# Two attention blocks on one core: a fixed order of work, B features read from PSUM, reciprocals by Ln and Exp, the first x tile turned on TensorE

## The chip, the cores and the metric

The kernel runs on one core of a Trainium2 chip. A time is device microseconds of that core, from the launch to the end; medians are of all runs of a series. A span is the profiled execution from its first to its last instruction, and is about 2 us shorter than the time of the same run. Some runs are marked slow (over 1.5% above the fastest run of the same kernel); ratios leave them out.

## The reference, cut to what matters

```python
def _A_ref(x, wqkv, wo):             # sliding window of 256, 32 heads of 20
    qkv = (x @ wqkv) ...             # B=1, S=2048, D=640
    scores = einsum("bhqd,bhkd->bhqk", q, k) * (Dh ** -0.5)
    mask = (i - j >= 0) & (i - j < 256)
    p = softmax(where(mask, scores, -1e9)); o = p @ v
    return o.reshape(B, S, D) @ wo

def _B_ref(x, wqkv, wo):             # linear attention, same sizes
    phi = lambda t: where(t > 0, t + 1, exp(t)) + 1e-6
    pq, pk = phi(q), phi(k)
    kv = einsum("bhsd,bhse->bhde", pk, v);  z = einsum("bhsd->bhd", pk)
    num = pq @ kv;  den = pq . z + 1e-6
    return (num / den).reshape(B, S, D) @ wo
# out = concatenate([A, B], -1), bf16
```

Block A needs 78 large exps of 128x2048 on ScalarE ("units" below), each fed by score matmuls into four PSUM banks (SC) and followed by mask products and P V matmuls. Block B is projections and small products. Its independent work is meant to fill TensorE while A waits.

## The kernel before

Every piece of work is an `op` with the engines that could run it. When the kernel is built, a greedy planner with a rough cost for each op chooses which engine runs what, and in which order each engine's stream is written. The parts that the change touches:

```python
# a group of matmuls into one of four PSUM banks FB[0..3]; the last op of evac gives the bank back
def group(mms, evac, key, ...): ...
def either(n): return {"DVE": dve_ps(n), "ACT": act_t(n)}     # planner's choice

# B features: copy out of PSUM, then exp and the max from SBUF
group(mms, [(either(HALF), lambda e, ps: copy(e, R1v[:, tb, ...], ps[:, 0:HALF]), ...)])   # x2 per block
def phi(dst, n, key, after, tag):
    # ACT:  e1 = exp(dst)
    # DVE:  e1 = min(e1, 1) + 1e-6                (tensor_scalar)
    # DVE:  dst = max(dst + 1 + 1e-6, e1)         (scalar_tensor_tensor)
    ...                                           # [cut]

# B denominators: VectorE add, four small transfers through DRAM, VectorE reciprocal
tensor_scalar_add(out=dsB, in0=ps, scalar1=1e-6)
dma d1 <- dsB[0:P:4];  dma rc <- d1;  reciprocal(rd, rc);  dma d2 <- rd;  dma rB <- broadcast(d2)

# x tiles: five transposing loads each, issued by the sync queue
q.dma_start_transpose(out=X[slot][:, c, :], in_=xsrc[which][t*NX:(t+1)*NX, c, :])

# masks: planner's choice
pl.op({"POOL": 0.25 + 0.002*4*w, "DVE": dve_sb(4*w)}, em, ...)
# [cut: everything else]
```

The softmax here doesn't subtract the row's maximum and nothing guards it: scores larger than these inputs give would overflow.

## Time and profile before

| | before |
|---|---|
| median time | 321.6 us (five runs, 318.5 to 327.2; 320.35 of three at the time of the prediction) |
| first exp starts / last exp ends | 25.96 / 283.79 us |
| busy: TensorE, VectorE, ScalarE, GpSimd | 264, 242, 198, 128 us |

First the page: busy time of the engines, then the busy share of TensorE, VectorE and ScalarE in 40 equal slices, in tenths.

```profile
PE 264.1 (82%) x4969; PEld 154.5 (48%) x5000; DVE 242.0 (76%) x495; ACT 197.9 (62%) x183; POOL 127.9 (40%) x150
...
PE   5257999979988878999989998986868687979593
...
DVE  7515565679998888658668268999999999987553
ACT  1004768648888877667775747888768875743100
```

Next the table of windows: start and end of a stretch, its length, then busy us and number of instructions for TensorE, its weight loads, VectorE, ScalarE and GpSimd, then granted clock, transfer share and GB/s. The first three stretches are head, middle and tail, cut at the first and the last exp; the last four are the part in which B's queries are made.

```profile
core 0: us, PE busy (x) PEld busy (x) DVE busy (x) ACT busy (x) POOL busy (x), PEclk, DMA share, GB/s
0.00:25.96 25.96, 13.00 (x56) 5.17 (x57) 11.96 (x29) 2.93 (x5) 11.54 (x28) 0.67 0.83 180
25.96:283.79 257.83, 223.80 (x4599) 130.87 (x4629) 209.49 (x420) 189.90 (x165) 106.90 (x105) 0.98 0.44 102
283.79:320.50 36.71, 27.33 (x316) 18.45 (x314) 20.58 (x47) 5.12 (x13) 9.43 (x18) 0.92 0.28 99
200.00:220.00 20.00, 16.44 (x319) 8.63 (x322) 19.45 (x39) 17.21 (x17) 8.56 (x9) 1.00 0.23 41
220.00:240.00 20.00, 15.18 (x302) 7.75 (x304) 19.96 (x37) 14.64 (x18) 11.85 (x11) 1.00 0.18 48
240.00:260.00 20.00, 15.66 (x434) 9.22 (x441) 19.97 (x43) 16.66 (x15) 9.43 (x11) 0.91 0.34 114
260.00:280.00 20.00, 16.70 (x417) 9.81 (x418) 19.36 (x40) 14.52 (x12) 10.45 (x12) 1.00 0.24 87
```

No engine bounds the whole span. In the middle TensorE has the most work (224 of 258 us), but in the last four rows VectorE is at 97 to 100% and TensorE at 76 to 84%.

The chain of waits, in order of time (start, length, what it was), shows the head: nine transposing loads, each issued by the sync queue (SPq) in 1.2 to 1.3 us, one after the other, then weights.

```profile
0.81 1.25 SPq L357
...
12.52 3.56 DMA R<-in_A_x_dram
...
16.10 5.54 DMA WV<-in_A_wqkv_dram
```

From the grouped view, the lines that the change removes or alters. After the bar: busy us, mean ns of one; after the second bar: the idle time of the engine just ahead of them, and who ended it.

```profile
L490 ACT ACTIVATE P<-SC 128x2048 bf16<-128x2048 f32 x78 | 146.4, 1877 | 51.0 <-PE SC L483 45.8 <-POOL P L513 3.5 <-issue 0.6
...
L319 DVE CAST R<-F 128x320 bf16<-128x320 f32 x35 | 16.6, 481 | 7.5 <-PE F L625 4.6 <-PE F L660 2.7
...
L653 DVE SCALAR_TENSOR_TENSOR R<-R,E 128x640 bf16<-128x640 bf16 x16 | 15.2, 947 | 0.1
...
L653 DVE SCALAR_TENSOR_TENSOR R<-R,E 128x512 bf16<-128x512 bf16 x10 | 8.9, 901 | 0.0
```

The large exps waited 45.8 us for scores. The SBUF form of the max (scalar-tensor-tensor) took 0.95 us for 640 elements in the mean. Of the 35 copies in the second line some are of output rows (those that waited for L625); these stay.

### The profile page before, as it was taken

What the parts mean: (1) busy time and instruction counts of PE and PEld (TensorE: products, weight loads), DVE (VectorE), ACT (ScalarE), POOL (GpSimd) and SP (SyncE); (2) the same over time, 40 slices, a digit from 0 to 9 for tenths busy, and PEclk for the clock granted to TensorE, in tenths of its full rate; (3) what the DMA queues carried; (4) which work ended last, traced back from release to release, by engine and by line L of the source; (5) the groups of instructions that cost most, each with busy time, mean ns of one, the idle gap of its engine ahead of it and who ended that gap; (6) DMA issues with size and microseconds to landing.
All of it is one profiled execution on the core that took longest, in us unless ns stands there. A gap on an engine that the chain in (4) does not pass through costs nothing.

```text
span 320.5 us, 11419 instructions
## 1 busy us (share of the span) xinstructions
PE 264.1 (82%) x4969; PEld 154.5 (48%) x5000; DVE 242.0 (76%) x495; ACT 197.9 (62%) x183; POOL 127.9 (40%) x150
## 2 busy tenths in 40 slices
PE   5257999979988878999989998986868687979593
PEld 1024454537544445565655864543435354546362
DVE  7515565679998888658668268999999999987553
ACT  1004768648888877667775747888768875743100
POOL 9500132430144535643435324272754564423232
PEclk9559999979999999999999979999999899999978
DMA  5896451844944541063509599400304222243221
GB/s 118 164 234 139 118 92 19 188 94 125 192 95 99 110 78 39 10 162 76 120 18 179 139 314 134 69 21 20 104 14 158 84 92 83 88 142 128 95 85 82
DMA packets 63028, 34.63 MB, mean 108 GB/s; under 512 B 52406, under 2 KB 59190, under 8 KB 62966
## 3 DMA queue, kind: packets, MB, share of 16 engines
q1 hardware_dynamic: 56194, 25.38, 35.2%
q0 software_dynamic: 1536, 5.24, 4.5%
q10 hardware_dynamic: 5248, 3.28, 4.3%
q8 instruction: 39, 0.64, 0.9%
q14 instruction: 11, 0.09, 0.1%
HBM read 15.50 MB, written 10.58 MB: 81 GB/s over the span
## 4 chain that ended last, share of the span: by engine, by line
DVE 39%; PE 30%; DMA 9%; issue 9%; SPq 6%; ACT 4%; POOL 2%; POOLq 0%; DVEq 0%; ACTq 0%
PE F L396 6%; PE F L424 6%; DMA RB<-RD 5%; PE F L660 5%; DVE RB L603 4%; DVE E L652 4%; PE F L669 4%; PE F L625 4%; DVE R L653 4%; ACT P L490 4%; SPq L357 4%; DVE P L513 3%; PE SC L483 3%; DVE ON L319 3%; DVE OT L604 3%
## 5 line engine op out<-in xcount | busy, mean ns | idle before, releaser
L490 ACT ACTIVATE P<-SC 128x2048 bf16<-128x2048 f32 x78 | 146.4, 1877 | 51.0 <-PE SC L483 45.8
L513 POOL TENSOR_TENSOR P<-P,MK 128x512 bf16<-128x512 bf16 (+1 forms) x90 | 98.6, 1105 | 147.2 <-ACT P L490 145.1
L483 PE MATMUL SC<-QK 20*64 20x128 bf16 (+4 forms) x1600 | 33.6, 253 | 4.7 <-ACT P L490 4.2
L513 DVE TENSOR_TENSOR P<-P,MK 128x512 bf16<-128x512 bf16 (+1 forms) x58 | 27.8, 486 | 5.9 <-ACT P L490 5.5
L660 PE MATMUL F<-W,X 128*128 128x320 bf16 x160 | 25.7, 313 | 4.8 <-DVE R L319 2.5
L729 PE MATMUL F<-X,XT 128*128 128x512 bf16 x94 | 23.9, 381 | 6.7 <-DVE G L319 1.5
L483 PEld LDWEIGHTS <-QK 20*64 20x64 bf16 x1600 | 15.6, 104 | 27.1 <-issue 25.9
L319 DVE CAST R<-F 128x320 bf16<-128x320 f32 (+1 forms) x43 | 22.0, 518 | 8.5 <-PE F L625 4.6
L572 PE MATMUL F<-P,V 64*32 64x64 bf16 (+4 forms) x2144 | 27.3, 226 | 0.9 <-issue 0.8
L319 DVE CAST QK<-F 128x512 bf16<-128x512 f32 x28 | 19.2, 687 | 11.2 <-PE F L396 10.9
L572 PEld LDWEIGHTS <-V 64*32 64x32 bf16 x2144 | 22.0, 91 | 11.3 <-issue 10.5
L396 PE MATMUL F<-X,WQ 128*128 128x512 bf16 x69 | 19.8, 398 | 7.6 <-DVE WQ L319 5.2
L424 PE MATMUL F<-WV,X 128*128 128x320 bf16 x120 | 20.0, 314 | 7.1 <-DMA WV<-in_A_wqkv_dram 3.3
L669 PE MATMUL F<-R,XT 128*128 128x320 bf16 x160 | 24.3, 300 | 0.0
L319 DVE CAST G<-F 128x320 bf16<-128x320 f32 (+2 forms) x30 | 14.3, 486 | 13.2 <-PE F L669 6.9
L653 DVE SCALAR_TENSOR_TENSOR R<-R,E 128x640 bf16<-128x640 bf16 (+1 forms) x26 | 24.0, 930 | 0.1
L396 PE MATMUL F<-X,WK 128*128 128x512 bf16 x63 | 19.0, 399 | 5.1 <-DVE WK L319 3.2
L603 DVE STREAM_SHUFFLE RB<-RB 128x512 f32<-128x512 f32 x32 | 22.1, 729 | 0.0
L660 PEld LDWEIGHTS <-X 128*128 128x128 bf16 x160 | 15.7, 102 | 12.7 <-issue 5.6
L651 ACT ACTIVATE E<-R 128x640 bf16<-128x640 bf16 (+1 forms) x26 | 17.6, 693 | 4.0 <-DVE R L319 3.9
L319 DVE CAST V<-F 128x320 bf16<-128x320 f32 x25 | 12.0, 489 | 10.3 <-PE F L424 10.1
L424 PEld LDWEIGHTS <-X 128*128 128x128 bf16 x120 | 11.8, 102 | 14.6 <-issue 8.9
(91 smaller groups left out, 370.6 us busy)
## 6 DMA issues: line engine op xcount, KB each, us to landing
QK<-dqk SPq DMA_DIRECT2D x6, 512.0 KB
XT<-in_B_x_dram SPq DMA_DIRECT2D x5, 512.0 KB
dqk<-QK SPq DMA_DIRECT2D x40, 48.0 KB
out_dram<-ST POOLq DMA_DIRECT2D x12, 160.0 KB, 2.3
out_dram<-G POOLq DMA_DIRECT2D x10, 160.0 KB, 2.1
out_dram<-R POOLq DMA_DIRECT2D x10, 160.0 KB, 2.1
do<-OS SPq DMA_DIRECT2D x6, 256.0 KB
WV<-in_A_wqkv_dram ACTq DMA_DIRECT2D x1, 800.0 KB
```

The source lines that it names most:

```text
L319: nc.vector.tensor_copy(out=dst, in_=src)
L396: mms.append((mm_t(NX), xkey(slot, k) + [("wqk", i, 0 if m == 0 else 1)], lambda ps, k=k: nc.tensor.matmul(ps[:], lhsT=WQK[i][:, k, m * P ...
L424: mms = [(mm_t(HALF), xkey(slot, k) + [("wv",)], lambda ps, k=k, hf=hf: nc.tensor.matmul(ps[:, 0:HALF], lhsT=X[slot][:, k, (kb % 4) * P : ...
L483: nc.tensor.matmul(SC[64 * rho : 64 * rho + 64, j, cc : cc + w], lhsT=QK[g][32 * j : 32 * j + Dh, kc : kc + 64], rhs=QK[g][32 * j : 32 * j ...
L490: nc.scalar.activation(out=pt[:], in_=SC[:], func=ACT.Exp, scale=scale)
L513: eng.tensor_tensor(out=pt[:, :, cc : cc + w], in0=pt[:, :, cc : cc + w], in1=MK[:, None, lo:hi].to_broadcast([P, 4, w]), op=ALU.mult)
L572: nc.tensor.matmul(FB[box[rg]][32 * j : 32 * j + 32, qc : qc + w], lhsT=V[kb % NV][64 * rho : 64 * rho + 64, HV * h : HV * h + 32], rhs=PT ...
L603: pl.op({"DVE": 0.62}, lambda e, c=c: nc.vector.stream_shuffle(out=RB[:, c], in_=RB[:, c], mask=[0] * 32), -2900, [("rb0",)], [("rb", rg)] ...
L653: return pl.op({"DVE": dve_ps(n)}, lambda e: nc.vector.scalar_tensor_tensor(out=dst, in0=dst, scalar=1.0 + 1e-6, in1=e1, op0=ALU.add, op1= ...
L660: mms = [(mm_t(HALF), [("x", slot, k), ("w1",)], lambda ps, k=k, b=b, hf=hf: nc.tensor.matmul(ps[:, 0:HALF], lhsT=X[slot][:, k, b * P : (b ...
L669: mms = [(mm_t(HALF), [("r1", tb), ("xt", c % 2)], lambda ps, tb=tb, c=c, hf=hf: nc.tensor.matmul(ps[:, 0:HALF], lhsT=XT[:, c % 2, tb, :], ...
L729: mms = [(mm_t(NX), [("x", slot, k)] + XK, lambda ps, k=k, c=c: nc.tensor.matmul(ps[:], lhsT=XW[:, k, :].rearrange("p (f c) -> p c f", c=K ...
```

## The change

Its intent is to take VectorE off the path of block B, to start the first matmuls sooner, and to replace the greedy choice by an order found beforehand. A table, `ORDER`, lists all 1382 ops as `number:engine` (with the PSUM banks where a matmul group takes some). D is VectorE, A ScalarE, P TensorE, G GpSimd, S the sync queue and Q ScalarE's queue. Every op is emitted where the table has it.

```diff
+ORDER = """
+5:S 0:G 16:Q 2:S 15:Q 8:S 14:Q 11:S 17:Q 19:Q 18:Q 23:S 3:P 6:P 20:Q 4:D 1:G 25:S 7:A 50:P:0 21:Q 9:P 51:D ...
+"""                                                            # [table cut]
-class Planner: ...                                             # [cut]
+class Graph:
+    def run(self, order):
+        for item in order.split():
+            ...; o.emit(engine)
-    FB = [psum.tile([P, NX], F32, name=f"F{i}") for i in range(4)]
+    FT = [psum.tile([P, NX], F32, name=f"F{i}") for i in range(4)]
+    FB = [t[:] for t in FT] + [SC[:, i, :] for i in range(4)]  # score banks too, once scores are done
-    E1 = [T([P, D], f"E{i}") for i in range(3)]
+    E1 = [T([P, NX], f"E{i}") for i in range(4)]
+    nc.scalar.preload_act_table_set("natural_log_exp_and_others")
+    def phi_evac(dst, n, wkeys):
+        return [
+            ({"ACT": act_ps(n)}, ... nc.scalar.activation(out=e1, in_=ps[:, 0:n], func=ACT.Exp) ...),
+            ({"DVE": dve_ts(n)}, ... nc.vector.tensor_scalar(out=e1, in0=e1, scalar1=1.0, scalar2=1e-6, op0=ALU.min, op1=ALU.add) ...),
+            ({"DVE": dve_ps(n)}, ... nc.vector.scalar_tensor_tensor(out=dst, in0=ps[:, 0:n], scalar=1.0 + 1e-6, in1=e1, op0=ALU.add, op1=ALU.max) ...)]
-        # den: VectorE add, d1, rc, VectorE reciprocal, d2, rB by four transfers
+        # den: lnB = Ln(ps + 1e-6);  rB = Exp(-lnB), both on ScalarE
+    def turn_x(tb, key):
+        # natural rows of the first x tile, 5 transposes by TensorE into SC, one copy to X[0]
-            pl.op({"POOL": 0.25 + 0.002 * 4 * w, "DVE": dve_sb(4 * w)}, ...)
+            pl.op({"DVE": dve_tt(4 * w), "POOL": 0.2 + 0.0019 * 4 * w}, ...)
+# [cut: weight columns copied per head group by VectorE or ScalarE, WV loaded in halves, ones set in V's columns only]
```

## The prediction

> **What bounds the kernel now.** The span is 320.5 us (the page); no engine bounds all of it. I cut it at the first exp (25 us) and after the last (283 us), by the table of windows.
>
> - Head, 0 to 25 us: VectorE 12.0 us busy, TensorE 12.0 (4.1 of it warm-up), granted clock 0.66. The chain of waits is nine x transposes issued one by one by the sync queue at 1.26 us each, then the WV load that lands at 21.7 us.
> - Middle, 25 to 283 us: TensorE 225 of 258 us, VectorE 209, ScalarE 190. The owner changes: TensorE is 97% busy at 40 to 60 and 140 to 160 us; from 200 to 280 us VectorE is 97 to 100% busy in every 20 us window, TensorE 76 to 84%. So the B query part is VectorE's.
> - Tail, 283 to 320.5 us: TensorE waits 3.5 us for the last relayed rows; output rows then leave at the pace of VectorE's casts (12.2 us for 76 matmuls that elsewhere cost 0.14 each).
>
> **What the change does**, costed with mean durations of the grouped view:
>
> - B features: 32 copies 128x320 and 20 copies 128x512 out of PSUM go (about 21 us VectorE, 7 ScalarE). The exp costs much as before. The scalar-tensor-tensor, 0.94 us for 640 from SBUF, becomes two of 0.48; at 512, 0.67 to 0.90 becomes 0.68: about 3 us saved. By the Trainium skill (SBUF — State Buffer, "Who interferes with whom") an op with two SBUF inputs competes with GpSimd, one with at most one does not; the spread 0.67 to 0.90 agrees.
> - B denominators: 4 adds, 4 reciprocals (6.5 us VectorE) and 16 small transfers go; 8 ScalarE passes of 0.6 come. By ScalarE: Activation LUTs ("Table sets: the hidden batching unit") exp and ln share a set, so no reloads.
> - Weight columns: 18 us VectorE becomes about 7 VectorE and 8 ScalarE.
> - Masks: VectorE could already take them (58 of 148); the table gives it 69: +5 us VectorE, -12 GpSimd. No gain in itself.
> - More evacuations go to ScalarE.
>
> The table's assignment, summed with these durations: TensorE 247 us at full clock, ScalarE 235 (was 198), VectorE 205 (was 242), GpSimd 114. Work is rebalanced; ScalarE becomes almost as loaded as TensorE. I cut the table at every fifth exp and took the busiest engine of each piece: 11 us to the first exp, 230 from there to the last, 21 after it.
>
> **The time.** First exp ends at about 20 us instead of 28 (natural x, transposes on TensorE, WV first). Middle 230 plus 5% for waits = 242. Tail 21 plus about 5 (store latency, relay wait) = 26. Sum 288 us. A fixed order can't adapt: where chip durations differ, three in-order engines wait for each other; that gives the upper side.
>
> Predicted 288 us, range 276 to 303. Faster by over 2%: 0.94; within 2%: 0.04; slower: 0.02.
>
> **What would show each step.** VectorE 200 to 212 us busy, ScalarE 228 to 240; feature casts and B reciprocal absent, one table load; scalar-tensor-tensor at 0.48 and 0.68; first exp starting before 21 us; no 20 us window of the B query part with VectorE over 90%; last exp done near 262 us; tail 24 to 29 us.
>
> **What would make it wrong.** ScalarE's waits for scores (52, 46 us in total) staying as large because more other work lies ahead of each exp; then 300 or more. A head still held by transfers (DMA share was 0.82 there). Table reloads. The other way: a well fitted order, middle 235, total near 277.

## The result, and the profile after

| | before | after |
|---|---|---|
| median time (five runs each) | 321.64 us | 301.01 us |
| ratio of the fast runs | 1 | 0.9408 (95% 0.9325 to 0.9491) |
| first exp starts | 25.96 us | 28.38 us |
| last exp ends | 283.79 us | 273.52 us |
| tail, from there to the end of the span | 36.7 us | 28.0 us |

A ratio is the mean time of one kernel's fast runs over that of the kernel before in the same rounds, so it is not quite the ratio of the medians. The result lies in the predicted range, 13 us above its centre.

The page, in the same lines as before:

```profile
PE 263.2 (87%) x5017; PEld 153.3 (51%) x5017; DVE 190.3 (63%) x429; ACT 222.7 (74%) x275; POOL 107.2 (36%) x153
...
PE   7069999978589999999999799798999999798883
...
DVE  1027532488986995936557246588998789877521
ACT  1038888898868899688887365888899998997331
```

The windows: head, middle, tail, and the four stretches of B's queries (columns as before).

```profile
0.00:28.38 28.38, 16.23 (x96) 8.68 (x97) 7.58 (x35) 8.41 (x25) 6.43 (x42) 0.76 0.94 215
28.38:273.52 245.14, 227.40 (x4655) 131.62 (x4654) 171.84 (x370) 204.18 (x226) 93.25 (x97) 0.98 0.44 99
273.52:301.50 27.98, 19.53 (x269) 12.95 (x267) 10.85 (x25) 10.12 (x25) 7.51 (x14) 0.95 0.29 107
200.00:220.00 20.00, 17.85 (x404) 10.02 (x404) 17.56 (x35) 17.20 (x17) 8.77 (x10) 1.00 0.47 129
220.00:240.00 20.00, 19.33 (x375) 10.88 (x374) 17.12 (x35) 18.60 (x23) 9.55 (x12) 1.00 0.14 50
240.00:260.00 20.00, 19.30 (x369) 11.11 (x370) 16.86 (x35) 18.77 (x22) 8.79 (x10) 1.00 0.15 52
260.00:280.00 20.00, 17.58 (x469) 11.19 (x469) 16.04 (x36) 16.80 (x25) 10.96 (x15) 1.00 0.29 99
```

VectorE lost 52 us of busy time and ScalarE gained 25. In the last four rows VectorE fell to 80 to 88% and TensorE rose to 88 to 97%. The middle shrank from 257.8 to 245.1 us (12.7 less), the tail from 36.7 to 28.0 (8.7 less, as 120 output matmuls instead of 170 are left after the last exp). The head grew by 2.4 us. These three make the 19.0 us between the two spans.

The grouped view of the same work: the copies of features and the reciprocal of B's denominators are gone, and the waits of the large exps for scores fell from 45.8 to 24.8 us.

```profile
L492 ACT ACTIVATE P<-SC 128x2048 bf16<-128x2048 f32 x78 | 146.8, 1882 | 26.9 <-PE SC L486 24.8 <-POOL P L513 1.2 <-PE F L570 0.4
...
L653 DVE SCALAR_TENSOR_TENSOR R<-F,E 128x320 bf16<-128x320 f32 x32 | 15.0, 480 | 0.6
...
L652 DVE TENSOR_SCALAR E<-E 128x320 bf16<-128x320 bf16 x32 | 12.3, 394 | 2.5 <-ACT E L651 2.3
...
L653 DVE SCALAR_TENSOR_TENSOR R<-F,E 128x512 bf16<-128x512 f32 x10 | 6.9, 689 | 0.3
```

The scalar-tensor-tensor takes 0.48 us for 320 elements with one operand in PSUM; all 32 lie between 0.43 and 0.49 us, whether GpSimd works beside them or not. The tensor-scalar beside it has its operands in SBUF and took 0.39 us in the mean. One of them took 0.97 us at 80.0 us, while GpSimd worked on mask products, and one 0.23 us at 71.0 us, where GpSimd was idle. The trace agrees with the Trainium skill, SBUF — State Buffer, "Who interferes with whom": a VectorE op with at most one SBUF input keeps out of GpSimd's way unless it runs in a mode that uses two ports, and tensor_scalar is named among the ops that can. u_e below is the test.

The head shows what the prediction missed. This is the timeline of TensorE (start, length, what; in brackets the idle time and who ended it):

```profile
5.08 0.82 PE L424 MATMUL SC<-ID,QK 128*128 128x128 bf16 x10
6.82 0.85 PE L410 MATMUL F<-WV,X 128*128 128x320 bf16 x5 [0.92 <-DVE X L300]
17.65 0.69 PE L424 MATMUL SC<-ID,QK 128*128 128x128 bf16 x5 [9.97 <-ACT X L296]
```

It made one group of five V matmuls at 6.8 us and then stood idle for 10 us, until ScalarE had copied the second turned block out of PSUM. This is ScalarE and its queue (ACTq) in the same time; L353, L356 and L362 are the weight loads of q and k:

```profile
6.44 6.16 ACTq L356 DMA_DIRECT2D R<-in_A_wqkv_dram  x2
...
16.48 0.38 ACTq L362 DMA_DIRECT2D R<-in_A_wqkv_dram  x1
16.90 0.69 ACT L296 CAST X<-SC 128x640 bf16<-128x640 f32 x1 [14.81 <-DMA X<-in_B_x_dram]
```

ScalarE did no work for 14.8 us before the copy "CAST X<-SC", though the input of this copy was ready at about 6 us, so that for some 11 of them the copy could have run. The compiled program (what the kernel builds to, not a trace) lists ScalarE's stream and the waits of each row:

```
5 L356 DMACopy R_102<-in_A_wqkv_dram 128x5x240 [waits DMAHW5_49]
6 L356 DMACopy R_102<-in_A_wqkv_dram 128x5x240 [waits DMAHW2_49]
7 L353 DMACopy R_102<-in_A_wqkv_dram 128x5x80 [waits DMAHW6_49]
8 L362 DMACopy R_102<-in_A_wqkv_dram 128x5x320 [waits DMAHW7_49]
9 L296 TensorCopy X_103<-SC 128x5x128 [waits DVE_49]
```

In this program eight completion semaphores (DMAHW0 to 7) serve the transfers of the sync queue and of ScalarE's queue, and a load is issued only when the last transfer with the same semaphore has landed. Rows 5 to 8 waited for such transfers, the last two of them for transposing loads of a B tile (B's first matmul that reads x starts at 58.0 us), and row 9, a copy, stands behind them in the same stream.

### The profile page after: what moved, and what is told of

The parts are those of the page before. It is cut to its first block, busy times and chain, and to the rows that moved or that the text cites. A ratio compares the mean times of both kernels' runs of the same rounds, so it can differ in the third digit from the quotient of the medians.

```text
span 301.5 us, 11480 instructions
## 1 busy us (share of the span) xinstructions
PE 263.2 (87%) x5017; PEld 153.3 (51%) x5017; DVE 190.3 (63%) x429; ACT 222.7 (74%) x275; POOL 107.2 (36%) x153
## 4 chain that ended last, share of the span: by engine, by line
PE 57%; DVE 16%; ACT 8%; DMA 7%; issue 5%; SPq 4%; POOL 1%; POOLq 0%; ACTq 0%; DVEq 0%
PE F L382 15%; PE F L668 8%; PE F L410 8%; PE F L626 7%; PE SC L486 6%; PE F L570 5%; ACT P L492 5%; PE F L725 3%; DVE E L652 3%; PE F L660 3%; SPq L341 3%; DVE R L653 2%; DMA R<-in_B_wo_dram 2%; DMA RC<-ON 2%; DVE RB L604 2%
## 5 line engine op out<-in xcount | busy, mean ns | idle before, releaser
L492 ACT ACTIVATE P<-SC 128x2048 bf16<-128x2048 f32 x78 | 146.8, 1882 | 26.9 <-PE SC L486 24.8
L513 POOL TENSOR_TENSOR P<-P,MK 128x512 bf16<-128x512 bf16 (+1 forms) x79 | 83.2, 1063 | 164.0 <-ACT P L492 164.0
L513 DVE TENSOR_TENSOR P<-P,MK 128x512 bf16<-128x512 bf16 (+1 forms) x69 | 32.9, 494 | 23.2 <-ACT P L492 22.9
L660 PE MATMUL F<-W,X 128*128 128x320 bf16 x160 | 26.5, 310 | 7.7 <-DVE R L653 7.4
L651 ACT ACTIVATE E<-F 128x320 bf16<-128x320 f32 (+1 forms) x52 | 24.9, 502 | 5.5 <-PE F L660 4.7
L486 PEld LDWEIGHTS <-QK 20*64 20x64 bf16 x1600 | 15.1, 104 | 25.7 <-issue 24.5
L725 PE MATMUL F<-X,XT 128*128 128x512 bf16 x100 | 25.7, 383 | 1.3 <-DVE R L653 1.0
L300 DVE CAST QK<-F 128x512 bf16<-128x512 f32 x22 | 15.1, 690 | 16.9 <-PE F L382 15.6
L652 DVE TENSOR_SCALAR E<-E 128x320 bf16<-128x320 bf16 (+1 forms) x52 | 21.5, 417 | 6.4 <-ACT E L651 6.1
L660 PEld LDWEIGHTS <-X 128*128 128x128 bf16 x160 | 15.5, 100 | 17.1 <-issue 9.9
L653 DVE SCALAR_TENSOR_TENSOR R<-F,E 128x320 bf16<-128x320 f32 (+1 forms) x42 | 21.9, 530 | 0.9
L668 PEld LDWEIGHTS <-XT 128*128 128x128 bf16 x160 | 15.3, 103 | 9.0 <-issue 1.2
L296 ACT CAST G<-F 128x320 bf16<-128x320 f32 (+2 forms) x25 | 10.4, 426 | 11.4 <-PE F L626 9.1
L300 DVE COPY ON<-F 128x512 f32<-128x512 f32 x21 | 13.8, 683 | 5.7 <-PE F L570 5.6
```

Of the source, the lines that this page charges most:

```text
L300: nc.vector.tensor_copy(out=dst, in_=src)
L486: nc.tensor.matmul(SC[64 * rho : 64 * rho + 64, j, cc : cc + w], lhsT=QK[g][32 * j : 32 * j + Dh, kc : kc + 64], rhs=QK[g][32 * j : 32 * j ...
L492: nc.scalar.activation(out=pt[:], in_=SC[:], func=ACT.Exp, scale=scale)
L513: eng.tensor_tensor(out=pt[:, :, cc : cc + w], in0=pt[:, :, cc : cc + w], in1=MK[:, None, lo:hi].to_broadcast([P, 4, w]), op=ALU.mult)
L652: ({"DVE": dve_ts(n)}, lambda e, ps: nc.vector.tensor_scalar(out=e1, in0=e1, scalar1=1.0, scalar2=1e-6, op0=ALU.min, op1=ALU.add), [("e1", ...
L660: mms = [(mm_t(HALF), [("x", slot, k), ("w1",)], lambda ps, k=k, b=b, hf=hf: nc.tensor.matmul(ps[:, 0:HALF], lhsT=X[slot][:, k, b * P : (b ...
```

## The experiments

Twelve kernels ran, all with correct results. They ran in four series on four chips: h0 to h3; f_b to f_bc with h4; u_b, u_d, u_e; u_b_late. Each series shares its runs of the kernel before, but only the first has a control, so h4 and the u runs are set against it by way of the kernel before. "First exp starts" comes from one profiled execution of each. "Ratio" is to the kernel before; below 1 is faster.

| run | what | median us | ratio (95%) | first exp starts |
|---|---|---|---|---|
| h0_after | changed kernel again | 302.6 | 0.9406 (0.933 to 0.948) | 27.3 |
| h1_turn_dve | two copies to VectorE | 299.6 | 0.936 (0.929 to 0.943) | 25.7 |
| h2_xb_late | B x loads later | 297.3 | 0.9293 (0.923 to 0.936) | 22.7 |
| h3_both | both | 298.3 | 0.9318 (0.925 to 0.938) | 24.2 |
| h4_head | both, in better order, and B's key weights later | 297.6 | 0.9242 (0.919 to 0.929) | 20.9 |
| f_b | before + B features from PSUM | 334.0 | 1.0364 (1.031 to 1.042) | 26.2 |
| f_c | before + Ln and Exp | 323.4 | 1.0014 (0.994 to 1.009) | – |
| f_bc | before + both | 330.5 | 1.0284 (1.022 to 1.035) | – |
| u_b | changed, features by the old path | 327.2 | 1.0144 (1.005 to 1.024) | 28.4 |
| u_b_late | changed, the copy kept but off ScalarE's path | 316.9 | 0.977 (0.970 to 0.984) | – |
| u_d | changed, first x tile by transposing loads | 306.1 | 0.9442 (0.932 to 0.956) | 28.5 |
| u_e | changed, all masks on GpSimd | 304.5 | 0.9463 (0.937 to 0.956) | 28.0 |

### The head: h0_after, h1_turn_dve, h2_xb_late, h3_both

The control has no edit (its table is only wrapped into lines differently).

> The changed kernel again, as the control of this series: ratio to the kernel before 0.94 (0.933 to 0.949), first exp starting near 28.4 us, TensorE idle for about 10 us between its first five V matmuls and the third transpose.

The ratio came out as expected, 0.9406. TensorE was idle for 8.2 us, and the first exp started at 27.3 us, against 10.0 and 28.4 in the execution of the same kernel shown above: so the start of the first exp differs by 1 us between two executions of one kernel.

```diff
-... 25:S 7:A 50:P:0 ...     # h1: copies of the 2nd and 4th turned block
+... 25:S 7:D 50:P:0 ...
-... 28:D 13:A 52:P:1 ...
+... 28:D 13:D 52:P:1 ...
```

> Only the second and fourth copies of the turned x tile move from ScalarE to VectorE. Theory A (the copy stands behind weight-load issues in ScalarE's in-order stream, and that is what holds the head): third transpose near 8 us instead of 17.7, TensorE's 10 us idle gone or cut to under 4, first exp 2 to 5 us earlier, total 297 to 300 (ratio 0.925 to 0.933). Theory B (the head is bound by how fast the transfers can bring weights; the copy is a symptom): V work moves earlier but the first exp stays within 1 us of 28.4 and the total within 1 us of the control, because q and k still wait for their weight columns.

The third transpose moved to 7.6 us. But the gap only moved, as TensorE's timeline shows:

```profile
7.64 0.44 PE L424 MATMUL SC<-ID,QK 128*128 128x128 bf16 x5
...
9.89 1.53 PE L410 MATMUL F<-WV,X 128*128 128x320 bf16 x10 [1.12 <-DMA WV<-in_A_wqkv_dram]
...
18.64 2.83 PE L410 MATMUL F<-WV,X 128*128 128x320 bf16 x10 [6.26 <-ACT V L296]
```

A V cast on ScalarE, behind the same weight loads, now held the bank for 6.3 us. The ten matmuls after the gap took 2.83 us at a granted clock of 0.50, where ten such matmuls before it, at 9.9 us, took 1.53 us at a clock of 1.00. The Trainium skill has this clock in TensorE: Matmul & The Clock Gate, "Part 1: The HAM clock gate": half rate by default and after an idle window, for which it gives about 3.4 us. The first exp came 1.6 us earlier than in the control, and the total fell by 1.5 us in the mean of fast runs, within the noise of both intervals; neither theory had foreseen this pair. Theory A is right about what held the copy, but what it was worth is at most a small gain that these runs do not separate from none.

```diff
-... 59:A 62:P:2 39:S ... 45:S ... 43:S ...         # h2: the ten B x loads (38 to 47), scattered
+... 176:A 39:S 45:S 43:S 46:S 42:S 40:S 38:S 41:S 44:S 47:S ...     # behind the fourth exp
```

> Only the ten transposing loads of the first two B x tiles move behind the fourth exp in the table. Theory A: ScalarE's copy is still behind the weight loads, but these are issued earlier, because no B transpose is ahead of them; a part of the idle goes (third transpose near 12 us), first exp 2 to 4 us earlier. Theory B (transfers bound the head): first exp 4 to 8 us earlier, 20 to 24 us, total 294 to 298, and the transfer share of the first 20 us still near 1 with the weights landing sooner. If B's keys now come too late, part of it is given back between 60 and 90 us.

The weight loads were issued sooner. ScalarE's timeline:

```profile
6.12 1.67 ACTq L356 DMA_DIRECT2D R<-in_A_wqkv_dram  x2
...
11.06 0.37 ACTq L362 DMA_DIRECT2D R<-in_A_wqkv_dram  x1
...
22.71 1.88 ACT L492 ACTIVATE P<-SC 128x2048 bf16<-128x2048 f32 x1 [0.67 <-PE SC L486]
```

The last loads of q and k weights left at 11.1 and 11.5 us instead of the control's 14.8 and 17.95; the first exp started at 22.7 us, 4.6 us before the control's, and the total fell by 3.6 us in the mean of fast runs (the two intervals just overlap). That is theory B, in the range that it expected, only that the transfer share of the first 20 us fell to 0.90 from 1.07. The copy on ScalarE waited less too (TensorE's gap is 4.1 us), so A and B are one thing: what waits is ScalarE's stream, and what it waits for are transfers. The ten B x loads can delay weights in two ways, as holders of the semaphores that weight loads wait for and as users of the transfer engines. This run takes away both, and no run parts them.

h3 is both edits.

> Both edits. Theory A alone: like the first edit, within 1 us. Theory B alone: like the second, within 1 us. If both hold: first exp at 19 to 22 us, total 291 to 296 (ratio 0.907 to 0.922), which is the head that the prediction assumed.

Not what either expected: 298.3 us, no better than h2. The trace says why. The fourth copy, now on VectorE, stands behind the copies of weight columns there and waited for their load (TensorE idle 3.9 us for it), the five V matmuls behind that took 1.52 us instead of 0.85, and the 800 KB of B's key weights, no longer held back in ScalarE's stream, left at 12.4 us instead of 17.7 (h2). That it competed with q's and k's weights is likely for a part of them only: with it moved as well (h4), k's first weight columns were copied at 13.6 us instead of 15.4, but q's second at 16.8 instead of 16.9.

### Mending the head: h4_head

```diff
 # h3, and:
-... 28:D 13:D ...            # weight columns, then the fourth copy
+... 13:D 28:D ...
-... 62:P:2 37:Q 22:S ...     # 800 KB of B's key weights
+... 44:S 47:S 37:Q ...       # behind the fourth exp, with the B x loads
```

> The changed kernel with the B x transposes and the 800 KB load of B's key weights behind the fourth exp, and the second and fourth copies of the turned x tile on VectorE, the fourth ahead of the weight-column copies. If the head is what the prediction missed: TensorE without a gap over 3 us after its first V matmul, first exp at 18.5 to 21 us, total 290 to 294 (ratio 0.903 to 0.915). If the query and key weight columns bound the head whatever the order: first exp again 22.5 to 24, total 296 to 298. If B's keys starve afterwards: a TensorE share under 70% between 60 and 80 us and the gain given back.

The first exp started at 20.9 us and TensorE's longest gap was 2.2 us. The windows of its head, middle and tail:

```profile
0.00:20.88 20.88, 15.21 (x95) 7.75 (x97) 9.46 (x37) 6.84 (x24) 6.43 (x42) 0.96 0.84 210
20.88:266.80 245.92, 224.81 (x4623) 131.62 (x4654) 171.05 (x370) 204.03 (x226) 92.53 (x97) 0.98 0.47 106
266.80:294.90 28.10, 19.51 (x268) 12.96 (x267) 10.86 (x25) 10.12 (x25) 7.52 (x14) 0.95 0.30 108
```

Its head is 7.5 us shorter than that of the changed kernel, while middle and tail are the same within a microsecond (245.9 and 28.1 us against 245.1 and 28.0). So in these two executions nearly all that the head gave came back in the span (6.6 of 7.5 us). The total is 297.6 us, ratio 0.9242: 5 us better than the control by the ratios (0.0164 times 322), short of the 290 to 294 us expected, which had asked for 8 us or more from a head that held 6 to 8. It is the total that was expected if q's and k's weight columns bound the head, and the trace shows them: on ScalarE the copy of q's weight columns waits for their load until 16.8 us.

```profile
16.76 1.40 ACT L296 COPY WQ<-R 128x400 bf16<-128x400 bf16 x6 [3.29 <-DMA R<-in_A_wqkv_dram]
```

It beats both kernels; against h2 it is not separated.

### What the parts of the change are worth: f_b, f_c, f_bc

These start from the kernel before, with its planner, and add one part.

```diff
-                ev.append(group(mms, [(either(HALF), copy out of PSUM)])); phi(...)     # f_b, and the same for queries
+                group(mms, phi_evac(R1v[:, tb, ...], HALF, [("r1", tb)]), ...)
-        # add, four transfers, reciprocal                                               # f_c
+        lnB = Ln(ps + 1e-6);  rB = Exp(-lnB)            # and the table set with both loaded at the start
```

> The kernel before, with its own planner, and of the change only the B features straight from PSUM (52 copies gone, scalar-tensor-tensor and exp read PSUM). Theory V (VectorE bounds the B query part, 200 to 280 us): about 14 us of VectorE work leave that stage and about 10 us the key stage; 8 to 14 us faster, ratio 0.955 to 0.975, VectorE busy near 220. Theory O (the gain is the order and the balance of engines in the table): within 1% of the kernel before, because the exps now hold PSUM banks longer until the last of three readers is done.

Both theories were wrong: it is 3.6% slower, though VectorE has 7 us less to do (235 us). Waits of TensorE (for whom: us in total, times, longest), before and then in this run; L660, L662 and L730 are B's projections, and L654 is the scalar-tensor-tensor:

```profile
PE SC L483 <- ACT P L490: 4.2, 8, 1.8
...
PE F L660 <- DVE R L319: 2.5, 4, 1.5
```

```profile
PE SC L483 <- ACT P L490: 11.8, 12, 2.1
PE F L662 <- DVE R L654: 8.0, 10, 2.1
...
PE F L730 <- DVE R L654: 3.4, 3, 1.5
```

Before, TensorE could reuse a bank when one copy had been made, by whichever of two engines the planner had chosen. Now it waits for the last of three ops on two engines in order, and 8.0 and 3.4 us of waits for it appear. Scores waiting for exps grew as well, from 4.2 to 11.8 us. That these waits are the loss is read from the trace, not tested: the planner also made another plan. It gave VectorE other work in place of most of the copies, so that VectorE lost 7 us and not the 24 expected. Between 200 and 280 us VectorE did get free, busy 52 to 88% instead of 97 to 100, but TensorE fell to 69 to 80%. What the planner would have done with better costs is not shown.

> The kernel before with its own planner and of the change only the reciprocal of the B denominators by Ln and Exp. Theory V: 6.5 us of VectorE leave its bounding stage, and four chains of four transfers go: 3 to 7 us faster, ratio 0.978 to 0.99. Theory O: within 1%.

No change (1.0014). The planner filled what was taken away: VectorE was busy 242.6 us, against 242.0 before. So this run tests whether the four chains of transfers were on the path (they were not) but not what 6.5 us off VectorE are worth.

> Both, still with the planner of before. Theory V: 12 to 20 us faster, ratio 0.94 to 0.963, so nearly the whole gain of the change (0.94) without its table, with VectorE under 93% between 200 and 270 us. Theory O: ratio above 0.98, and the table makes the rest.

2.8% slower, with VectorE at 231 us in all and at 52 to 92% between 200 and 280 us. So with the old planner the two parts gain nothing; they cost.

### Undoing parts within the table: u_b, u_d, u_e, u_b_late

```diff
-  nc.scalar.activation(out=e1, in_=ps, func=Exp)                                             # u_b
+  nc.vector.tensor_copy(out=dst, in_=ps); nc.scalar.activation(out=e1, in_=dst, func=Exp)
-  scalar_tensor_tensor(out=dst, in0=ps, ...)
+  scalar_tensor_tensor(out=dst, in0=dst, ...)
```

> The changed kernel with its table, but B's features take the old path again: a VectorE copy out of PSUM, exp and scalar-tensor-tensor from SBUF. VectorE busy 190 to about 216. If VectorE has slack in the table everywhere: at most 3 us slower than the control (ratio 0.94 to 0.95). If VectorE's latency is on the path of the B stages: 8 to 15 us slower (ratio 0.965 to 0.99).

Slower than either theory had it: ratio 1.0144, about 24 us above the control (0.0738 times 322). VectorE has only 212 us. What is new is a wait of ScalarE for VectorE's copies, ahead of the exps in its stream, 32.3 us in the three lines (the control has none):

```profile
ACT E L651 <- DVE R L651: 23.4, 34, 2.4
...
ACT E L651 <- DVE WQ L651: 4.6, 4, 1.8
ACT E L651 <- DVE WK L651: 4.3, 4, 1.8
```

With the fixed table nothing on ScalarE can pass such a wait, and the large exps stand behind it. To part the load from the handover, u_b_late keeps the 52 copies on VectorE but puts them behind the exp:

```diff
-  tensor_scalar(out=e1, in0=e1, ...)                         # u_b_late; the exp reads PSUM again
+  nc.vector.tensor_copy(out=dst, in_=ps); tensor_scalar(out=e1, in0=e1, ...)
-  scalar_tensor_tensor(out=dst, in0=ps, ...)
+  scalar_tensor_tensor(out=dst, in0=dst, ...)
```

> The changed kernel with its table; the exp reads PSUM as in the change, but the VectorE copy out of PSUM stays, placed behind the exp, and the scalar-tensor-tensor reads SBUF. VectorE carries the same 52 copies as in the run u_b (busy about 212 us), but ScalarE no longer waits for VectorE ahead of its exp. Theory H (u_b lost its 25 us through the added handover VectorE to ScalarE, which holds up ScalarE's in-order stream): ratio 0.94 to 0.96, and ScalarE's waits for VectorE's copies (23 us in u_b) are gone. Theory L (it lost them through VectorE's load, 21 us more in the stages that bound it): ratio 1.0 to 1.02, as u_b.

```profile
ACT E L651 <- DVE R L653: 5.2, 4, 2.3
```

It came out between the two: 0.977, with VectorE at 214 us. ScalarE's waits for VectorE ahead of these exps fell from 32.3 to 5.2 us (0.3 in the control). So by estimate about half of u_b's loss, 0.0374 of 0.0738 or 12 us, is the handover, and the other half, 0.0364 or 12 us, is what 52 copies on VectorE cost otherwise. The second half is not the load alone: each copy also makes its bank free later, and the 5.2 us of waits are in it. VectorE is nearly full again, though, at 80 to 100% in the four windows between 200 and 280 us. The runs are of three series, with the kernel before as the link, and by the intervals of the ratios each half is uncertain by about 4 us.

```diff
-  q.dma_start(out=src[:, tb, :], in_=A_x[0][rows of tb])                                     # u_d
+  q.dma_start_transpose(out=X[0][:, c, :], in_=xsrc["A"][0:NX, c, :])      # c of five, over the four ops
-  five transposes into SC;  copy(e, X[0][...], SC)
+  pass
```

> The changed kernel with its table, but the first x tile comes by five transposing loads again and TensorE turns nothing. If turning on TensorE gains what the prediction said: the first V matmul moves from 7 us to 10 or later, first exp 2 to 4 us later, 2 to 4 us slower than the control. If the turn gains nothing because its copies wait in ScalarE's stream and the weights come late in any case: first exp within 1 us or earlier, total within 2 us of the control.

First exp at 28.5 us, as with the turn; ratio 0.9442, not separated from the control. TensorE began V at 5.8 us even so. No gain of the turn shows in this head: here too the chain to the first exp runs through ScalarE's stream, where a V cast stands behind the last weight load, issued at 20.5 us. With the head of h4 it was not tried.

```diff
-... every mask op with :D ...        # u_e, 69 of them
+... :G ...
```

> The changed kernel with all 148 mask products on GpSimd: GpSimd busy 107 to about 180, VectorE 190 to about 158. The prediction called the mask assignment no gain in itself: then within 3 us of the control, as GpSimd still has 120 us free. If the table needs the masks on VectorE for their latency (0.5 against 1.1 us ahead of the P V products): 5 us or more slower, with P V matmuls or exps waiting for GpSimd.

Ratio 0.9463, not separated from the control by its interval; GpSimd is busy 170 us, VectorE 174. If the choice of engine for masks is worth anything, it is under 2%.

VectorE was expected at 158 us. About half of the difference, 8 us, is the tensor-scalars in SBUF: with more work on GpSimd their mean rose from 394 to 533 ns at 320 elements, while the scalar-tensor-tensors that read PSUM stayed at 480.

```profile
L652 DVE TENSOR_SCALAR E<-E 128x320 bf16<-128x320 bf16 x32 | 16.8, 533 | 9.1 <-ACT E L651 8.8
```

## Why the prediction was right, and which of its terms was off

- **Busy times.** VectorE was put at 200 to 212 us and ScalarE at 228 to 240; they were 190 and 223. The sums of mean durations were too high: instructions in a row overlap in the trace (an ACTIVATE that starts at 256.64 and lasts 0.68 is followed by one at 257.21), so the busy time is less than the sum. Summed in the same way (count times mean), the trace after gives 211 for VectorE and 239 for ScalarE, close to the 205 and 235 predicted; the error was to set these sums beside the busy times before (242 and 198; the sums before are 278 and 204). The shift of load was right in sign: 52 us off VectorE where the prediction had 37, 25 on to ScalarE where it had 37.
- **The middle.** "Middle 230 plus 5% for waits = 242", counted from the end of the first exp. Measured 243.3 (30.26 to 273.52). Right: the busiest engine of each piece, plus a little.
- **No VectorE window over 90%, scalar-tensor-tensor at 0.48 and 0.68, one table load, score waits falling.** All seen: 88% at most, 0.480 and 0.689, one load, 45.8 to 24.8 us. The Trainium skill's ScalarE: Activation LUTs, "Table sets: the hidden batching unit", was right that exp and ln share a set.
- **The tail.** "21 plus about 5 = 26"; measured 28.0.
- **The head: the term that failed.** "First exp ends at about 20 us instead of 28 (natural x, transposes on TensorE, WV first)." It ended at 30.3 us, which is 10 of the 13 us missed (1 more came in the middle and 2 in the tail; the 2 us by which a time is longer than its span are cancelled by the profiled run, which was 2 us above the median). I had named the cause under "what would make it wrong" (a head held by transfers, as 0.82 of the transfer time was used there) and still counted the gain. What the runs showed in its place: weight loads are issued from ScalarE's stream, each waits for an earlier transfer, and ScalarE's copies wait behind them (h1). The transfers in question are ten B x loads that nobody needs yet (h2). With these and the B key weights moved away the first exp starts at 20.9 us (h4), where the prediction wanted it, and 5 us of the 13 come back. That the result lies in the range all the same is in part luck: the upper side was argued from engines that wait for each other in the middle, which kept to its estimate, and the head used it up.
- **Why it gained: half right.** The prediction said that VectorE bounds the B query part and that relief of VectorE gives the gain. In the table this fits about 12 us (u_b_late). But it also read the gain of each part as its work taken off the bounding engine, and that does not hold by itself: with the old planner the same edit made the kernel 3.6% slower, although VectorE got free between 200 and 280 us (f_b). The Ln and Exp did nothing (f_c), but there VectorE was not relieved. The gain needs the table and the short path together. How much the table alone would gain, without the PSUM path but with an order found for that, no run shows; u_b is the old path in an order made for the new one.

## What to carry to other kernels

Taking work off the busiest engine pays only if the order lets the others use it: a bank that is given back after three ops instead of one, or a copy put ahead of an op on another in-order engine, can cost more than the work saved. A load issued from a compute engine's stream is an instruction that can wait, and all compute behind it waits too, so put loads that nobody needs yet behind those that everybody needs (h2), and consider a queue without compute for early loads that must wait (not tried here). Estimate a phase at the start from what must land before its first instruction, not from its compute.

## What the Trainium skill lacked or had wrong

- DMA: Bandwidth & Descriptors, "Issuing engines are not separate DMA queues": it says that issuing from several engines saves only the sequencer's issue time. It stops short of the cost: a load waiting to be issued in a compute engine's stream holds that engine's compute. Here ScalarE stood idle for 14.8 us before a 0.69 us copy, some 11 of them with the copy's input ready, and TensorE 10.0 us for the copy.
- Trace Analysis ("Perfetto Trace Analysis", "Optimizing Scalar/DVE Operations"): it says that with VectorE saturated, moving some work to ScalarE may make sense. It lacks what a handover between the two costs when nothing in a stream can pass a wait: by estimate 12 us for 52 copies ahead of ScalarE's exps (1.0144 against 0.977).
- Nothing in the passages used here was found wrong by these runs.
